# A list scheduler given other instruction costs, router constants moved to an earlier due time, and the state rows of heads 3 to 5 exchanged

## The chip, the core and the metric

The kernel runs on one core of a Trainium2 chip. The metric is the device time of one execution in microseconds. Five engines work side by side, each on its own queue in program order: PE (matrix multiplications; PEld is its weight load), DVE (vector), ACT (scalar, with function tables), POOL (which here issues the indirect transfers) and SP (which issues almost all other transfers). Engines wait for one another by semaphores.

## The reference

The reference is one linear recurrence with a complex decay per head, followed by two mixtures of experts. Cut to what matters:

```
# 4 x 8 heads, 768 steps, 48 channels; a is complex, its size clipped at 0.999
for t in range(768):
    S_re, S_im = a_re*S_re - a_im*S_im + outer(k[t], v[t]),  a_re*S_im + a_im*S_re
    y[t] = q[t] @ S_re
x = y, heads side by side                                  # 3072 tokens x 384
# MoE 1: a token with x @ w_skip > 0 goes to the best of 8 experts
x += gate * (relu(x @ w1[e]) @ w2[e]),  e = argmax(x @ w_gate)
# MoE 2: every token goes to the best of 8 experts
logits = normalise(x) @ normalise(expert_emb).T / tau
out = gate * (relu(x @ w1[e]) @ w2[e]),  e = argmax(logits) # w1 384 x 1024, w2 1024 x 384
```

## The kernel before

**How it is recorded.** No instruction is issued where it is written. Each is recorded in a `Plan` (L72 to 240) with its engine, a modelled cost, what it reads and writes, and a due time; a transfer also has a modelled time in flight. Dues are carried backwards through the dependences. Then forward and backward list-scheduling passes run over the modelled times, and the order with the shortest modelled end is issued. So a modelled cost is not a time on the chip, but it decides the order in every engine's queue. Modelled idle time of PE is filled with dummy matrix multiplications (`keep_warm`, L431).

**The recurrence (about 0 to 250 us).** The work is cut into eight groups `g` (a batch and half of its sequence) and 24 chunks of 128 tokens. `feat(g)` (L440 to 552) loads the decay (tile RI) and q with k (tile QK, L463). On ACT and DVE it turns the decay into running sums (scans, L471) and into sine and cosine. Two multiplications (L529) give tile PR (the cosine part of q and k) and, in place, tile QK (the sine part). Both are then moved on chip (L540) into tile ST, where a head's cosine part and sine part stand under one another in 96 partitions. PIECES lists the five moves for each part: heads 0 to 2, heads 3 to 5, and three for heads 6 and 7. `chunk(k)` (L575 to 690) multiplies on PE from ST (W, L593), masks on DVE (WM, L596), turns k round (KT, L604), makes the output (L620) and the state (L629), and then x with the first router's scores (L640 to 646).

**Between.** Router constants (`consts`, L771 to 812): five small loads, the expert embeddings' norms on DVE, two tiny matrix multiplications (L805, L806) and three small DVE operations (L809 to 811), which the first chunk's scores need. `route` ranks tokens and scatters them by POOL into a table `tab` in device memory (L733); `slots` (L758) reads back two lanes of it (ts1f and LANE for MoE 1; ts2f and LANE for MoE 2).

**The experts.** `gather` (L995) has POOL gather up to 128 rows of x into one of twelve buffers xg. PE turns them round (L919), DVE or ACT copy them (L925, L926), h = relu(x w1) is L950 with L954 and L958, o = h w2 is L982. Weights are loaded by SP (w1 at L884, w2 at L887) into a few buffers r and split into high and low parts (ACT L893, DVE L894). MoE 1 scatters its result into xd (L1036), MoE 2 into out (L1231). In MoE 2, `select` (DVE, L1150 to 1153) computes each expert's slot indices, and the expert number goes to SP by a cast on POOL (WE, L873).

```
PIECES = [((0, 3), 0, 0, 0, 48), ((3, 6), 0, 48, 0, 48), ((6, 8), 0, 96, 0, 32), ((6, 7), 2, 96, 32, 16), ((7, 8), 2, 112, 32, 16)]
# (heads, block, source partition, row within the part, rows)
for x, ks, a0 in ((vp, kp, 0), (vc, kqk, 1)):      # PR is part 0, QK part 1
    ...  d[a0 * D + o : a0 * D + o + m, ...] <- x[p0 : p0 + m, ...]     # D = 48
```

Of the kernel before, what the change touches and what calls it, by code (L numbers as in the profile page):

```python
# [15 lines left out]
ALU = mybir.AluOpType  # L16
AX = mybir.AxisListType
# [4 lines left out]
P = 128  # L22
# [47 lines left out]


def cells(g):  # L72

    return PARTS.get(g, ((0, NC),))


class Plan:
# [9 lines left out]

    def add(self, eng, cost, fn, r=(), w=(), due=1e9, lat=0.0, tab=None, phase=None, dram=None, after=()):
# [20 lines left out]
        self.ops.append([eng, cost, fn, deps, due, lat, tab, self.bias, dram, self.hold])  # L109

    def lag(self, i, j):
        a, b = self.ops[i], self.ops[j]
        if b[3][i] is None:
            return 0.0
        if a[5]:
            return self.START + a[5] + self.END
        if a[0] != b[0]:
            return self.CROSS
        return self.SAME if b[3][i] and a[0] != "pe" else 0.0
# [16 lines left out]
    def forward(self, due, succ):  # L136
# [11 lines left out]
        while len(out) < n:  # L148
# [29 lines left out]
            if o[5]:  # L178
                dma = max(dma, end + self.START) + o[5]
                done = dma + self.END  # L180
                late = done - end - (self.START + o[5] + self.END)
# [11 lines left out]
    def backward(self, ends, succ):  # L193
# [10 lines left out]
        while count < n:  # L204
# [15 lines left out]
            if o[5]:  # L220
                flight = self.START + o[5]
                late = max(lanes[eng][0] + flight + self.END, dma + flight)
                if o[8]:
                    a, b = o[8]
                    late = max([late] + [touched.get((a, c), -9.0) + flight + self.END for c in self.CLASH[b]])
# [48 lines left out]
def kernel(  # L274
# [112 lines left out]
    def dve(n, fn, r, w, due=1e9):  # L387
        plan.add("dve", 0.06 + 1.05e-3 * n, fn, r, w, due)

    def pe(us, fn, r, w, due=1e9):  # L390
        plan.add("pe", us, fn, r, w, due)

    def dma(us, fn, r, w, due=1e9, dram=None, cost=0.47):
        plan.add("sp", cost, fn, r, w, due, us, dram=dram)

    def pool(us, fn, r, w, due=1e9, dram=None):
        plan.add("pool", 1.05, fn, r, w, due, us, dram=dram)

# [34 lines left out]
    def feat(g):  # L433
# [72 lines left out]
        def back(i, j):  # L506
# [30 lines left out]
            for x, ks, a0 in ((vp, kp, 0), (vc, kqk, 1)):  # L537
                for y, (h, bk, p0, o, m) in enumerate(PIECES):
                    nh = h[1] - h[0]
                    dma(MOVE * wide(j) / P * nh * m / D, lambda x=x, a0=a0, h=h, nh=nh, bk=bk, p0=p0, o=o, m=m: nc.sync.dma_start(  # L540
                        d[a0 * D + o : a0 * D + o + m, 2 * h[0] * w : 2 * h[1] * w],
                        x[p0 : p0 + m, 2 * bk * w : 2 * (bk + nh) * w]),
                        ks(j), [("st", g % 2, y, a0, i) for i in range(j.start, j.stop)], cost=0.64)
# [134 lines left out]
    def route(nm, n, nr, lg, klg, sel, ksel, c0, pay, kpay, inval, pcol, due, late=(), pt0=0):  # L678
# [52 lines left out]
        for i in range(n):  # L731
# [3 lines left out]
                in_=pay[:, i, 0:W], in_offset=None, bounds_check=2 * E * N - 1, oob_is_err=False),  # L735
                [("ix", nm)] + klg + kpay + span(["ti"], range(2), (0, E // 2), [lane]), [("tab", nm, i)] + ([("tabB", lane)] if late else []), due, (f"t{lane}", "all"))
        tabs.append([("tab", nm, i) for i in range(n)])
# [20 lines left out]
    def slots(t, view, src, ks, key, due, kf=()):  # L758
        parts = [view(x) for x in t["l"]]
        for lane in range(2):  # L760
            dma(0.2, lambda lane=lane: nc.sync.dma_start(parts[lane], src(lane)), ks, [(key, lane), *kf], due, (f"t{lane}", "read"))
        dve(math.prod(parts[0].shape[1:]), lambda: nc.vector.tensor_tensor(view(t["f"]), parts[0], parts[1], op=ALU.add), [(key, 0), (key, 1)], [(key, 2), *kf], due)
# [64 lines left out]
    feat(0)()  # L827
    pe(0.5, lambda: nc.tensor.matmul(PS[7][:, 384:512], lhsT=PR[:, 0:P], rhs=maskT, start=True, stop=True), [("pr", 0, 0)], [], -100.0)
    consts()
    feat(1)()  # L830
    backs = {}
# [98 lines left out]
    def h_part(m, e, cap, c0, c1, due, raw=False):  # L930
# [4 lines left out]
        cut = [(c0, cap - rem), (cap - rem, c1)] if c1 == cap and rem else [(c0, c1)]  # L935
        us = 0.66 * w / P if raw else 9 * max(w, 250) / 2370
        for f in range(NF):
# [25 lines left out]
    def o_part(m, e, cap, c0, c1, due, finish, raw=False):  # L963
# [3 lines left out]
        for t in range(c0 // P, -(-c1 // P)):  # L967
# [3 lines left out]
            for f0, f1 in ((0, 6), (6, 8)):  # L971

                def mm(f0=f0, f1=f1, t=t, n=n, po=po):
# [11 lines left out]

                pe(0.488 * (f1 - f0) * (1 if n == P else 0.667), mm,
                   span([name], range(f0, f1), [min(t, 2)], range(2) if n == P else (0, 2)) + span(["w2"], range(f0 // 2, f1 // 2), range(2)),
# [3 lines left out]
    def gather(m, e, t, n, idx, kidx, kx, due, rows=N + 1):  # L991
        s = slot(m, e, t)
        if rows <= N:
# [3 lines left out]
            in_offset=IO(ap=idx.bitcast(U32), axis=0), bounds_check=rows - 1, oob_is_err=False),  # L997
            kidx + kx + ["w"], [("xg", s), ("xgd", m, e, t)], due, ("x", "read") if rows > N else None)

# [3 lines left out]
    def moe1():  # L1003
# [20 lines left out]
        def finish(e, t, n, po, kpo, due):  # L1024
# [13 lines left out]
                in_=T["o"][ox], in_offset=None, bounds_check=N - 1, oob_is_err=False),  # L1038
                [("o", ox)] + kx, [("xs", e, t)], due + 4, ("x", "all"))
            bank = 3 if t % 2 else 6  # L1040
# [104 lines left out]
    def select(p, h, kin, due):  # L1145
# [6 lines left out]
        dve(144, lambda: V.tensor_reduce(f, tmp, axis=AX.X, op=ALU.add), kin + [("tmp", h)], [("f2", p % 3, h)], due)  # L1152
        dve(2, lambda: V.tensor_scalar(
# [53 lines left out]
    def moe2():  # L1207
# [12 lines left out]
        def finish(p, t, n, po, kpo, due):  # L1220
# [5 lines left out]
            else:  # L1226
# [6 lines left out]
                in_=T["o"][ox][0:n], in_offset=None, bounds_check=N - 1, oob_is_err=False),  # L1233
                [("o", ox)], [("out", p, t)], due + 4)

# [7 lines left out]
        def gates2(p, t0, t1, k, due):  # L1243
# [6 lines left out]
            for t, r in tiles(p)[t0:t1]:  # L1250
                x = slot(1, p, t)
                act(508, lambda t=t, r=r, x=x: nc.scalar.activation(  # L1252
                    T["xg"][x][0:r], T["xg"][x][0:r], AF.Square, accum_out=SQ2[0:r, i0 + t : i0 + t + 1]),
# [316 lines left out]
```

## Time and profile before

| what | value |
|---|---|
| runs | 709.4, 713.12, 712.95 us; median 712.95 |
| profiled execution, its own time | 710.47 us |
| its span, first to last instruction | 708.7 us |
| mean granted clock of PE | 0.945 |
| PE busy | 631.4 us (89%) |
| DVE, ACT, POOL busy | 459.9 (65%), 401.5 (57%), 163.9 (23%) us |
| moved by DMA | 115.91 MB, mean 164 GB/s |

The profiled execution lasted 1.8 us more than its span. A high share of PE over the whole says little about a single stretch: the recurrence, the two passages into the mixtures and the mixtures themselves have different limits, so the rows below go by stretches. [...]

### The profile page before, as it was taken

Reading aid. Unit: us, or ns where it says so; the run is one execution under the profiler, and the core shown is the slowest. Engines: PE = TensorE matmul, PEld = TensorE weight load, DVE = VectorE, ACT = ScalarE, POOL = GpSimd, SP = SyncE. Lnnn points to the kernel's source line nnn. Section 1 sums busy time; section 2 is a strip of 40 time slices with the busy share of each in tenths; the row PEclk is TensorE's granted clock in tenths of the full one; section 3 lists DMA queues with packets and bytes.
Section 4 is the critical chain, followed back from the end, with each engine's and each line's share of the span. In section 5 each row is a group of like instructions: output and inputs, shape, how many; then the busy total and the mean of one; then the engine's idle time right before and its main releaser. Section 6 shows DMA issues by size and latency. Waiting matters only on the chain.

```text
span 708.7 us, 12836 instructions
## 1 busy us (share of the span) xinstructions
PE 631.4 (89%) x4734; PEld 606.7 (86%) x4734; DVE 459.9 (65%) x1058; ACT 401.5 (57%) x695; POOL 163.9 (23%) x171
## 2 busy tenths in 40 slices
PE   0478999799989987799999999859999999999995
PEld 0478988788979877799999999859999999999995
DVE  4997899699986463667676747726836536374350
ACT  6986979587976532555555544215654535555340
POOL 5000000000344225212332134544141413102101
PEclk9996999699999998799999999857999999999998
DMA  9866997599566777756455331494554433023001
GB/s 296 307 172 158 297 247 183 151 220 232 129 155 156 264 193 258 242 195 215 138 143 152 103 107 20 82 347 143 179 198 143 156 112 134 33 89 115 30 10 36
DMA packets 52103, 115.91 MB, mean 164 GB/s; under 512 B 22909, under 2 KB 27139, under 8 KB 49346
## 3 DMA queue, kind: packets, MB, share of 16 engines
q1 hardware_dynamic: 43682, 93.94, 46.2%
q0 software_dynamic: 8352, 21.09, 9.4%
q8 instruction: 39, 0.64, 0.4%
q14 instruction: 30, 0.25, 0.1%
HBM read 83.30 MB, written 14.09 MB: 137 GB/s over the span
## 4 chain that ended last, share of the span: by engine, by line
PE 58%; DMA 13%; DVE 11%; issue 10%; SPq 3%; POOL 2%; ACT 2%; POOLq 0%; DVEq 0%; ACTq 0%
PE PS L982 23%; PE PS L950 23%; DMA ST<-QK 4%; DMA tab<-LG,ixa 3%; PE PS L919 2%; PE PS L593 2%; DMA ST<-PR 2%; DMA QK<-in_qk 2%; POOL tab L733 2%; DMA LANE<-tab 1%; SPq L540 1%; PE PS L431 1%; DVE WM L596 1%; PE PS L620 1%; DVE RI L471 1%
## 5 line engine op out<-in xcount | busy, mean ns | idle before, releaser
L950 PE MATMUL PS<-x,w 128*128 128x256 f32 (+4 forms) x1152 | 188.5, 323 | 7.8 <-DVE zn L748 7.8
L982 PE MATMUL PS<-w,h 128*128 128x384 f32 (+1 forms) x1032 | 190.9, 340 | 0.0
L950 PEld LDWEIGHTS PS<-x,w 128*128 128x128 f32 x1152 | 179.4, 200 | 9.6 <-issue 7.9
L982 PEld LDWEIGHTS PS<-w,h 128*128 128x128 f32 (+1 forms) x1032 | 177.5, 185 | 2.7
L954 ACT ACTIVATE h<-PS 128x256 fp32r<-128x256 f32 (+5 forms) x136 | 58.0, 428 | 119.5 <-PE PS L950 97.6
L958 DVE SCALAR_TENSOR_TENSOR h<-PS,h 128x256 fp32r<-128x256 f32 (+4 forms) x184 | 67.7, 391 | 76.1 <-ACT h L954 57.4
L593 PE MATMUL PS<-ST 96*128 96x128 f32 x384 | 60.5, 303 | 14.2 <-DMA ST<-QK 9.7
L593 PEld LDWEIGHTS PS<-ST 96*128 96x128 f32 x384 | 52.6, 210 | 17.9 <-DMA ST<-QK 10.2
L1231 POOL DMA_INDIRECT out<-o,ts2i x30 | 29.7, 991 | 165.0 <-ACT o L1225 118.7
L900 DVE TENSOR_TENSOR w<-r,w 128x768 fp32r<-128x768 f32 x64 | 58.4, 951 | 13.3 <-ACT w L899 10.1
L926 DVE TENSOR_TENSOR x<-PS,x 128x256 fp32r<-128x256 f32 (+4 forms) x48 | 23.1, 485 | 56.7 <-ACT x L925 52.0
L899 ACT CAST w<-r 128x768 fp32r<-128x768 f32 x64 | 50.5, 832 | 15.5 <-PE PS L982 8.3
L894 DVE TENSOR_TENSOR w<-r,w 128x1024 fp32r<-128x1024 f32 x45 | 53.5, 1219 | 5.0 <-ACT w L893 5.0
L925 ACT CAST x<-PS 128x256 fp32r<-128x256 f32 (+4 forms) x48 | 20.3, 426 | 54.1 <-PE PS L919 47.9
L431 PE MATMUL PS<-cst 128*128 128x128 f32 x302 | 45.4, 300 | 3.0 <-DVE cs L810 1.8
L893 ACT CAST w<-r 128x1024 fp32r<-128x1024 f32 x45 | 45.0, 1050 | 0.3 <-issue 0.2
L431 PEld LDWEIGHTS PS<-cst 128*128 128x128 f32 x302 | 41.5, 213 | 4.2 <-DVE cs L810 1.9
L995 POOL DMA_INDIRECT xg<-xd,ts2i x30 | 34.7, 1157 | 35.3 <-ACT xg L1252 17.6
L558 POOL DMA_DIRECT2D VT<-in_v x8 | 4.6, 572 | 162.2 <-PE PS L620 112.9
L596 DVE TENSOR_TENSOR WM<-PS,cst 128x512 f32<-128x512 f32 x48 | 32.2, 679 | 12.3 <-PE PS L593 12.1
L620 PE MATMUL PS<-WM,VT 128*48 128x128 f32 x384 | 37.9, 288 | 1.1 <-DVE WM L596 0.8
L733 POOL DMA_INDIRECT tab<-LG,ixa x24 | 27.8, 1158 | 47.6 <-DMA tab<-LG,ixa 23.3
(209 smaller groups left out, 960.7 us busy)
## 6 DMA issues: line engine op xcount, KB each, us to landing
r<-in_w1a SPq DMA_DIRECT2D x24, 512.0 KB
r<-in_w2a SPq DMA_DIRECT2D x32, 384.0 KB
r<-in_w1b SPq DMA_DIRECT2D x24, 512.0 KB
r<-in_w2b SPq DMA_DIRECT2D x32, 384.0 KB
RI<-in_ri SPq DMA_DIRECT2D x6, 1152.0 KB
QK<-in_qk SPq DMA_DIRECT2D x6, 1152.0 KB
ST<-PR SPq DMA_DIRECT2D x12, 432.0 KB
ST<-QK SPq DMA_DIRECT2D x12, 432.0 KB
```

The costliest lines, as they stand in the source:

```text
L431: nc.tensor.matmul(PS[7][:, 384:512], lhsT=ident, rhs=maskT, start=True, stop=True)
L593: nc.tensor.matmul(wt[:, h % 4, :], lhsT=st(1, h), rhs=st(0, h), start=True, stop=True)
L620: nc.tensor.matmul(py[64 * j : 64 * j + D, p, :], lhsT=w, rhs=r, start=(x == 0), stop=(x == 1 or i == 0))
L733: pool(0.2, lambda i=i, lane=lane: nc.gpsimd.indirect_dma_start(out=tab[lane][:, :], out_offset=IO(ap=ix[:, i : i + 1].bitcast(U32), axis= ...
L893: act(F, lambda s=s: nc.scalar.copy(T["w1"][q % 2][0][s], T["r1"][q % 2][s]), [("r1", q % 2, j), "L"], [k + (0,)])
L894: dve(F, lambda s=s: nc.vector.tensor_tensor(T["w1"][q % 2][1][s], T["r1"][q % 2][s], T["w1"][q % 2][0][s].bitcast(F32), op=ALU.subtract), ...
L899: act(2 * DM, lambda s=s: nc.scalar.copy(T["w2"][0][s], T["r2"][s]), [("r2", j)], [k + (0,)])
L900: dve(2 * DM, lambda s=s: nc.vector.tensor_tensor(T["w2"][1][s], T["r2"][s], T["w2"][0][s].bitcast(F32), op=ALU.subtract), [("r2", j), k + ...
L950: nc.tensor.matmul(ph, lhsT=l, rhs=r, start=(i == 0), stop=(i == len(seq) - 1))
L954: act(w, lambda f=f, ph=ph: nc.scalar.activation(T[name][:, f, o0 : o0 + w], ph, AF.Relu), [("ps", f % 3), "w" if name == "hA" else "L"], ...
L958: dve(b - a, lambda f=f, ph=ph, a=a, b=b, o=o: nc.vector.scalar_tensor_tensor(T[name][:, f, o : o + b - a], ph[:, a - c0 : b - c0], 0.0, T ...
L982: nc.tensor.matmul(po if n == P else po[0 : 2 * stride], lhsT=x, rhs=w[:, f, :], start=(f == 0 and i == 0), stop=(f == NF - 1 and i == len ...
```

## The change

Five things change, most of them numbers of the scheduler's model.

1. `row(h, k)`: for heads 3 to 5 the cosine part goes to rows 48 to 95 of ST and the sine part to rows 0 to 47. The other heads stay: cosine in rows 0 to 47, sine in rows 48 to 95. Both factors of each product are moved alike, so the products are the same.
2. `consts()` is recorded with a bias of -60 on its due times.
3. The modelled costs: a POOL issue 0.6 instead of 1.05 and an indirect one 1.3; a DVE operation 0.07 + 1.045e-3 n instead of 0.06 + 1.05e-3 n; the selections 250 and 240 elements instead of 144; h_part 9 * (w / 2400 + 0.0135) instead of 9 * w / 2370; o_part 0.52 for each step instead of 0.488; a square of ACT 430 instead of 508.
4. A new term `more` in the modelled time in flight: 1.2 for a table scatter and a slot load, 2.0 for a gather.
5. What follows from these numbers: another order in all five queues, with the same real work. Dummy multiplications also fall in other places.

```diff
+def row(h, k):
+    return (1 - k if h[0] == 3 else k) * D
...
         if a[5]:
-            return self.START + a[5] + self.END
+            return self.START + a[5] + self.END + a[10]
...
-        plan.add("dve", 0.06 + 1.05e-3 * n, fn, r, w, due)
+        plan.add("dve", 0.07 + 1.045e-3 * n, fn, r, w, due)
...
-    def pool(us, fn, r, w, due=1e9, dram=None):
-        plan.add("pool", 1.05, fn, r, w, due, us, dram=dram)
+    def pool(us, fn, r, w, due=1e9, dram=None, cost=0.6, more=0.0):
+        plan.add("pool", cost, fn, r, w, due, us, dram=dram, more=more)
...
-                        d[a0 * D + o : a0 * D + o + m, 2 * h[0] * w : 2 * h[1] * w],
+                        d[row(h, a0) + o : row(h, a0) + o + m, 2 * h[0] * w : 2 * h[1] * w],
...
+    plan.bias = -60.0
     consts()
+    plan.bias = 0.0
...
-        us = 0.66 * w / P if raw else 9 * max(w, 250) / 2370
+        us = 0.66 * w / P if raw else 9 * (max(w, 250) / 2400 + 0.0135)
...
-            kidx + kx + ["w"], [("xg", s), ("xgd", m, e, t)], due, ("x", "read") if rows > N else None)
+            kidx + kx + ["w"], [("xg", s), ("xgd", m, e, t)], due, ("x", "read") if rows > N else None, 1.3, 2.0)
...
-        dve(144, lambda: V.tensor_tensor(
+        dve(250, lambda: V.tensor_tensor(
```

Three places in the queues. The first is the beginning of PE's queue (dg and tt are the router constants, cst a constant, the rows of L431 dummies). Before, the rows that led up to the constants, in the middle of the first chunks' work:

```order
L593 MATMUL PS_101<-ST_108 128x128 x4
L604 MATMUL PS_103<-cst,ST_108 128x96 x4
L431 MATMUL PS_107<-cst 128x128 x3
L593 MATMUL PS_100<-ST_108 128x128 x4
L620 MATMUL PS_104<-WM_112,VT_120 48x128 x4
L620 MATMUL PS_104<-WM_113,VT_120 48x128 x4
L604 MATMUL PS_102<-cst,ST_108 128x96 x4
L593 MATMUL PS_100<-ST_108 128x128 x4
L805 MATMUL PS_107<-dg,cst 128x8
L806 MATMUL PS_107<-tt,cst 128x1
```

and now, from the head of the queue (line numbers are 5 higher here):

```order
L810 MATMUL PS_107<-dg,cst 128x8
L811 MATMUL PS_107<-tt,cst 128x1
L436 MATMUL PS_107<-cst 128x128 x9
L833 MATMUL PS_107<-cst,PR 128x128
L436 MATMUL PS_107<-cst 128x128 x41
L609 MATMUL PS_102<-cst,ST_108 128x96 x4
L598 MATMUL PS_100<-ST_108 128x128 x4
```

The two matrix multiplications of the constants moved from behind the first chunk's work to the head of the queue.

The second is SP's queue at the entry of MoE 1, where the weights of the next expert (w1a into r) meet the slot loads from the table. Before:

```order
L645 DMA xd<-XT_123 128x384
L884 DMA r_2255<-in_w1a 128x1024 x3
L761 DMA ts1f<-tab_64 128x7x9
L761 DMA LANE<-tab_65 128x7x9
L761 DMA ts1f<-tab_64 128x7x9
L761 DMA LANE<-tab_65 128x7x9
L884 DMA r_2255<-in_w1a 128x1024 x3
```

and now:

```order
L650 DMA xd<-XT_123 128x384
L891 DMA r_2241<-in_w1a 128x1024 x5
L766 DMA ts1f<-tab_64 128x7x9
L766 DMA LANE<-tab_65 128x7x9
L766 DMA ts1f<-tab_64 128x7x9
L766 DMA LANE<-tab_65 128x7x9
L891 DMA r_2241<-in_w1a 128x1024
```

Two of the later weight loads, which need a buffer that a split (L894) sets free, now stand ahead of the slot loads.

The third is POOL's queue at the entry of MoE 2 (the last table scatters, the scatter of finished rows to out, the gathers). Before:

```order
L733 DMA tab_64<-LG,ixb_203 49152x17
L733 DMA tab_65<-LG,ixb_204 49152x17
L1231 DMA out<-o_2036,ts2i 3072x384
L995 DMA xg_2030<-xd,ts2i 128x384
L995 DMA xg_2031<-xd,ts2i 64x384
L995 DMA xg_2034<-xd,ts2i 128x384
L995 DMA xg_2035<-xd,ts2i 64x384
L995 DMA xg_2032<-xd,ts2i 128x384
```

and now:

```order
L738 DMA tab_64<-LG,ixb_203 49152x17
L738 DMA tab_65<-LG,ixb_204 49152x17
L1238 DMA out<-o_1986,ts2i 3072x384
L1238 DMA out<-o_1987,ts2i 3072x384
L1002 DMA xg_1980<-xd,ts2i 128x384
L1002 DMA xg_1981<-xd,ts2i 64x384
L1002 DMA xg_1982<-xd,ts2i 128x384
L1002 DMA xg_1983<-xd,ts2i 128x384
```

A second scatter to out came ahead of the first gather; the weights' cast WE still follows the sixth gather.

## Rows read from the trace of the kernel before

**Rows 1.** Windows: busy us (count) of PE, PEld, DVE, ACT, POOL; clock, DMA share, GB/s.

```profile
20.00:40.00 20.00, 12.01 (x82) 12.01 (x83) 19.96 (x25) 19.03 (x22) 0.00 (x0) 1.00 0.76 273
...
120.00:140.00 20.00, 15.13 (x103) 14.15 (x102) 13.55 (x18) 12.48 (x14) 0.53 (x1) 0.66 0.71 176
...
250.00:300.00 50.00, 40.08 (x277) 38.39 (x277) 26.10 (x92) 19.83 (x47) 18.68 (x18) 0.86 0.74 233
300.00:340.00 40.00, 40.00 (x299) 39.85 (x299) 26.18 (x53) 20.77 (x38) 9.65 (x10) 1.00 0.58 186
...
440.00:498.00 58.00, 47.99 (x255) 44.68 (x254) 33.25 (x131) 19.77 (x50) 26.41 (x26) 0.76 0.64 188
498.00:700.00 202.00, 202.00 (x1136) 195.79 (x1134) 101.32 (x249) 97.61 (x202) 40.70 (x39) 1.00 0.31 104
```

**Rows 2.** Waits of DVE from 20 to 200 us: total, times, longest.

```profile
DVE WM L596 <- PE PS L593: 8.5, 5, 2.8
DVE QK L515 <- ACT T L501: 3.4, 2, 1.7
DVE rt L809 <- PE PS L806: 2.1, 1, 2.1
```

**Rows 3.** Chain that ended last, 0 to 300 us: start, microseconds, what.

```profile
46.11 6.01 DMA ST<-PR
...
142.40 8.75 DMA ST<-PR
...
153.51 8.74 DMA ST<-QK
...
280.70 5.06 issue
```

**Rows 4.** PE at the entry of MoE 2, idle time before in brackets.

```profile
459.29 5.43 PE L950 MATMUL PS<-x,w 128*128 128x192 f32 x27
472.49 3.91 PE L950 MATMUL PS<-x,w 128*128 128x192 f32 x17 [7.77 <-DVE zn L748]
```

**Rows 5.** Window of the long idle time there.

```profile
461.00:472.00 11.00, 3.72 (x21) 3.55 (x20) 0.08 (x1) 0.33 (x1) 7.50 (x10) 0.66 0.99 371
```

**Rows 6.** SP's moves into ST in two groups: start, microseconds, what.

```profile
112.96 4.83 SPq L540 DMA_DIRECT2D ST<-PR  x4
117.89 3.63 SPq L540 DMA_DIRECT2D ST<-QK  x3
...
141.15 5.57 SPq L540 DMA_DIRECT2D ST<-PR  x5
```

**Rows 7.** Windows of 4 us around those moves, and one with loads.

```profile
116.00:120.00 4.00, 4.00 (x55) 3.71 (x54) 4.00 (x6) 2.44 (x7) 0.00 (x0) 1.00 1.00 171
120.00:124.00 4.00, 2.84 (x27) 2.65 (x26) 4.00 (x8) 4.00 (x4) 0.53 (x1) 1.00 0.99 209
144.00:148.00 4.00, 4.00 (x56) 3.69 (x54) 2.31 (x3) 3.97 (x5) 0.00 (x0) 1.00 0.96 171
148.00:152.00 4.00, 3.57 (x34) 3.30 (x34) 4.00 (x8) 3.49 (x5) 0.00 (x0) 1.00 0.95 230
...
80.00:84.00 4.00, 3.88 (x41) 3.69 (x40) 3.90 (x2) 4.00 (x8) 0.00 (x0) 1.00 1.01 397
```

**Rows 8.** SP at the entry of MoE 1: slot loads, then weights.

```profile
260.56 0.38 SPq L761 DMA_DIRECT2D ts1f<-tab  x1
...
263.75 13.02 SPq L884 DMA_DIRECT2D r<-in_w1a  x6
```

**Rows 9.** POOL at the entry of MoE 1, idle time before in brackets.

```profile
271.89 1.03 POOL L995 DMA_INDIRECT xg<-xd,ts1i  x1 [6.40 <-DMA xd<-o,ts1i]
```

**Rows 10.** POOL's first two gathers of MoE 2.

```profile
450.50 1.26 POOL L995 DMA_INDIRECT xg<-xd,ts2i  x1 [0.44 <-issue]
452.07 0.98 POOL L995 DMA_INDIRECT xg<-xd,ts2i  x1 [0.31 <-DVE ts2i L1153]
```

**Rows 11.** ACT's second output of MoE 2.

```profile
452.47 0.58 ACT L1225 ACTIVATE o<-PS,ts2g 128x384 f32<-128x384 f32 x1 [3.65 <-issue]
```

More of the change, by code (lines that the diff above doesn't have):

```diff
@@ L86, in __init__, with add @@
         self.bias, self.hold, self.phases = 0.0, 0.0, {}
-    def add(self, eng, cost, fn, r=(), w=(), due=1e9, lat=0.0, tab=None, phase=None, dram=None, after=()):
+    def add(self, eng, cost, fn, r=(), w=(), due=1e9, lat=0.0, tab=None, phase=None, dram=None, after=(), more=0.0):
         i = len(self.ops)
@@ L108, in add @@
             self.phases.setdefault(phase, []).append(i)
-        self.ops.append([eng, cost, fn, deps, due, lat, tab, self.bias, dram, self.hold])
+        self.ops.append([eng, cost, fn, deps, due, lat, tab, self.bias, dram, self.hold, more])
     def lag(self, i, j):
@@ L179, in forward @@
                 dma = max(dma, end + self.START) + o[5]
-                done = dma + self.END
-                late = done - end - (self.START + o[5] + self.END)
+                done = dma + self.END + o[10]
+                late = done - end - (self.START + o[5] + self.END + o[10])
                 lanes[eng] = lanes[eng][1:] + [done]
@@ L221, in backward @@
                 flight = self.START + o[5]
-                late = max(lanes[eng][0] + flight + self.END, dma + flight)
+                late = max(lanes[eng][0] + flight + self.END + o[10], dma + flight)
                 if o[8]:
                     a, b = o[8]
-                    late = max([late] + [touched.get((a, c), -9.0) + flight + self.END for c in self.CLASH[b]])
+                    late = max([late] + [touched.get((a, c), -9.0) + flight + self.END + o[10] for c in self.CLASH[b]])
                 if late > t:
@@ L387, in dve, with dma @@
     def dve(n, fn, r, w, due=1e9):
-        plan.add("dve", 0.06 + 1.05e-3 * n, fn, r, w, due)
+        plan.add("dve", 0.07 + 1.045e-3 * n, fn, r, w, due)
     def pe(us, fn, r, w, due=1e9):
         plan.add("pe", us, fn, r, w, due)
-    def dma(us, fn, r, w, due=1e9, dram=None, cost=0.47):
-        plan.add("sp", cost, fn, r, w, due, us, dram=dram)
-    def pool(us, fn, r, w, due=1e9, dram=None):
-        plan.add("pool", 1.05, fn, r, w, due, us, dram=dram)
+    def dma(us, fn, r, w, due=1e9, dram=None, cost=0.47, more=0.0):
+        plan.add("sp", cost, fn, r, w, due, us, dram=dram, more=more)
+    def pool(us, fn, r, w, due=1e9, dram=None, cost=0.6, more=0.0):
+        plan.add("pool", cost, fn, r, w, due, us, dram=dram, more=more)
     st_s, el_s, st_w, st_l = (ExitStack() for _ in range(4))
@@ L735, in route @@
                 in_=pay[:, i, 0:W], in_offset=None, bounds_check=2 * E * N - 1, oob_is_err=False),
-                [("ix", nm)] + klg + kpay + span(["ti"], range(2), (0, E // 2), [lane]), [("tab", nm, i)] + ([("tabB", lane)] if late else []), due, (f"t{lane}", "all"))
+                [("ix", nm)] + klg + kpay + span(["ti"], range(2), (0, E // 2), [lane]), [("tab", nm, i)] + ([("tabB", lane)] if late else []), due, (f"t{lane}", "all"), 1.3, 1.2)
         tabs.append([("tab", nm, i) for i in range(n)])
@@ L760, in slots @@
         for lane in range(2):
-            dma(0.2, lambda lane=lane: nc.sync.dma_start(parts[lane], src(lane)), ks, [(key, lane), *kf], due, (f"t{lane}", "read"))
+            dma(0.2, lambda lane=lane: nc.sync.dma_start(parts[lane], src(lane)), ks, [(key, lane), *kf], due, (f"t{lane}", "read"), more=1.2)
         dve(math.prod(parts[0].shape[1:]), lambda: nc.vector.tensor_tensor(view(t["f"]), parts[0], parts[1], op=ALU.add), [(key, 0), (key, 1)], [(key, 2), *kf], due)
@@ L984, in mm @@
                                 stop=(f == NF - 1 and i == len(seq) - 1))
-                pe(0.488 * (f1 - f0) * (1 if n == P else 0.667), mm,
+                pe(0.52 * (f1 - f0) * (1 if n == P else 0.667), mm,
                    span([name], range(f0, f1), [min(t, 2)], range(2) if n == P else (0, 2)) + span(["w2"], range(f0 // 2, f1 // 2), range(2)),
@@ L1038, in finish @@
                 in_=T["o"][ox], in_offset=None, bounds_check=N - 1, oob_is_err=False),
-                [("o", ox)] + kx, [("xs", e, t)], due + 4, ("x", "all"))
+                [("o", ox)] + kx, [("xs", e, t)], due + 4, ("x", "all"), 1.3)
             bank = 3 if t % 2 else 6
@@ L1149, in select @@
         oh = OH[:, p, :].rearrange("p (a b e) -> p a b e", a=1, b=1).to_broadcast([P, 2, E + 1, E])
[L1150 removed]
+        dve(250, lambda: V.tensor_tensor(
             tmp, src, oh, op=ALU.mult), kin + [("oh2", min(p, 1))], [("tmp", h)], due)
[L1152 removed]
+        dve(240, lambda: V.tensor_reduce(f, tmp, axis=AX.X, op=ALU.add), kin + [("tmp", h)], [("f2", p % 3, h)], due)
         dve(2, lambda: V.tensor_scalar(
@@ L1233, in finish @@
                 in_=T["o"][ox][0:n], in_offset=None, bounds_check=N - 1, oob_is_err=False),
-                [("o", ox)], [("out", p, t)], due + 4)
+                [("o", ox)], [("out", p, t)], due + 4, None, 1.3)
         def gathers(p, due, t0=0):
@@ L1251, in gates2 @@
                 x = slot(1, p, t)
-                act(508, lambda t=t, r=r, x=x: nc.scalar.activation(
+                act(430, lambda t=t, r=r, x=x: nc.scalar.activation(
                     T["xg"][x][0:r], T["xg"][x][0:r], AF.Square, accum_out=SQ2[0:r, i0 + t : i0 + t + 1]),
```

## Prediction

> **What bounds the kernel now.** I read the windows by stage first, because the whole hides the stages [rows 1]. In the mixtures PE is the bound: 40.00 of 40 us from 300 to 340 and 202.00 of 202 from 498 to 700, at full clock. The change takes no real work out of them, so nothing can be won there but dummies. From 20 to 40 us DVE is the bound (19.96 of 20). From 120 to 140 nothing is: PE 15.13, DVE 13.55, at a mean clock of 0.66. The two passages, 250 to 300 and 440 to 498, keep PE busy 40.08 of 50 and 47.99 of 58 us, at clocks of 0.86 and 0.76.
>
> The waits of DVE from 20 to 200 us come next [rows 2]: 8.5 us in five waits for the first product of a chunk (WM behind L593), 3.4 us for ACT, and 2.1 us for the router's tiny products (rt behind L806). The first product needs tile ST, and the chain of waits says the same: moves into ST lie in it from 46.11 us on, with 6.01, 8.75 and 8.74 us in the rows shown [rows 3].
>
> In the passages the chain ends in PE standing for something that no instruction explains: 5.06 us at 280.70 [rows 3], 7.77 us before 472.49 [rows 4]. In the second, the eleven microseconds from 461 have DVE busy 0.08 and ACT 0.33 us, while the DMA engines are busy 0.99 at 371 GB/s [rows 5]: gathers and weight loads together.
>
> **The change part by part.** The profiled execution took 710.47 us, its span 708.7 us. The sum is made against 710.47; the median of the runs is 2.5 us higher and their lowest 1.1 us lower, so one profile does not fix the level better than that.
>
> *Rows of heads 3 to 5.* Before, SP issued the cosine moves (PR, all into rows 0 to 47) as one batch and the sine moves (QK, all into rows 48 to 95) as another [rows 6]. The windows of 4 us over them show DMA engines equally busy, 0.95 to 1.00, but with different yields [rows 7]: 171 GB/s in both windows that hold PR moves, 209 and 230 GB/s in the two after them, when QK moves follow; 397 GB/s with loads alone. So a busy engine does not mean a given rate, and the target rows seem to decide it. A group's PR batch is two pieces of 48 x 2304, one of 32 x 1536 and two of 16 x 768 numbers of 4 bytes, 1.18 MB: 6.9 us at 171 GB/s, 5.4 us at the mean of 220, a gain of 1.5 us. Other transfers share the windows and blur the difference, so I take 2 us a group.
> [...]
> A landing that is earlier by 2 us helps only where someone waits. The stretch from 120 to 140 alone has 6.45 us of idle DVE [rows 1], so that most of the five waits of 8.5 us [rows 2] hang on one landing; I estimate that they shrink by its 2 us, what lies elsewhere by 2 us too, and by 0.5 us more as PE's half clock in that stretch ends sooner. That makes -4.5 us, with bounds of 0 (DVE is the bound and fills the time anyway) and -8.5 (all five waits). QK moves lose nothing by it: their batch now has the same mix of rows.
>
> *Router constants.* Their products moved to the head of PE's queue. The wait of 2.1 us [rows 2] goes, and DVE's small operations for them move ahead of the first multiplications (L529). There DVE is the bound [rows 1], and they push these back by as much; but it is the same work, only earlier. I take -1.5 us; bounds -2.1 and +1 (the first landing of 46.11 to 52.12 us later [rows 3]).
>
> *Entry of MoE 1.* SP now issues two more loads of 512 KB ahead of the slot loads. At 397 GB/s [rows 7] that is 1.3 us each, 2.6 us on slots that were issued from 260.56 [rows 8]. But the gathers did not wait for slots: the first was issued at 271.89 after 6.40 us of waiting for a scatter to xd [rows 9], which lay beside six weight loads that held SP 13.02 us [rows 8]. Of these loads, two now come earlier. I take 0, bounds +2.6 (the slots' delay in full) and -2.6 (the scatter lands earlier by as much).
>
> *Entry of MoE 2.* POOL's first gather was issued at 450.50 [rows 10]. It now stands behind the second scatter to out, whose rows ACT ends at 452.47 + 0.58 = 453.05 [rows 11]. With 1.0 us for the scatter, as for a gather, and the gap of 0.3 us [rows 10] the gather comes at 454.4, 3.9 us later. PE's first expert product, 459.29 [rows 4], came 7.2 us after the second gather at 452.07; part of that was DVE, busy with selections that will by then be done, so I count +2 us of the 3.9. Behind the gather wait all later gathers and the cast that gives SP the expert number, so the burst of loads moves back about 4 us as well, and the long idle time with it. Bounds: -7.8 (the idle time of 7.77 us goes) and +9.3 (third rival).
>
> *Modelled costs.* They cost nothing on the chip. The rest of the order in the mixtures changes little, and PE covers it [rows 1]: 0, give or take 1 us.
>
> Sum: -4.5 - 1.5 + 0 + 2 + 0 = -4.0 on 710.47. **Forecast 706.5 us.** About 0.5%, 3.6 us, is what a measurement of this kernel can tell from no change: below 709.4 counts as faster than the median of 712.95, above 716.5 as slower.
>
> **Rivals.**
> *Phase one gains nothing.* The moves' yield hangs on the transfers that share the windows rather than on rows, or DVE fills the time. For it: DVE is busy 19.96 of 20 us [rows 1]; the 171 and 209 GB/s lie only a fifth apart [rows 7]. Against it: the chain holds ST moves of over 8 us [rows 3], and DVE does wait for them. Then -1.5 + 2, 711 us.
> [...]
> *The idle time at 461 us goes or shrinks.* Gathers, moved later by 4 us, and weight loads no longer fill the engines together. For it: the order around is another. Against it: POOL issues the same six gathers before the cast, and the weights follow the cast as before. Then -4.5 - 1.5 - 7.8, and about 1.7 us less at half clock afterwards (an estimate): 695 us.
> *Slower: PE meets the idle time with nothing done.* The first gather comes at 454.4. If the engines then fill up before its rows are turned, the 27 products of 5.43 us that ran from 459.29 [rows 4] run after the idle time, at half clock: 3.9 + 5.4 = +9.3 us. This decides if the first expert product starts after the stall does. With a gain of 2 to 3 us in the first phase it gives 710.5 + 9.3 - 2.5 = 717 us. For it: eleven idle microseconds are already there [rows 5], and the change takes nothing away from the burst. Against it: the burst hangs on the same queue and moves back as well.
>
> **How the numbers follow.** Forecast 0.45, no gain in phase one 0.22, idle time gone 0.13, slower 0.20. Within the forecast the bounds above give 701 to 711. Faster is most of the forecast (0.36), all of the idle time's case (0.13) and a little of the second (0.04): 0.53. Slower is most of the last rival (0.16) and 0.06 from the upper bounds of both entries coming together in the other cases: 0.22. Within 0.5% is what is left: 0.25. The range reaches from the 695 of the second rival to the 717 of the third, 695 to 717, with about 2 in 10 outside.
>
> **What would show it.** PR moves: windows over them above 200 GB/s, and landings in the chain under 7 us. Constants: no wait of rt behind L811. WM's waits for L598 under 5.5 us in all from 20 to 200. Entry of MoE 1: the first gathers of the burst not later, against the end of the recurrence, than 271.89. Entry of MoE 2: first gather 4 us behind its place, relative to the last products of MoE 1, and the idle time still about 8 us. The prediction is wrong if the landings are as long as before, or if the idle time before MoE 2 changes by more than 3 us in either direction.

## The result, and the profile after

The change made the kernel slower: 718.77 us (median of 20 runs) against 710.6 us for before in the same comparison, ratio 1.0108 [1.0079, 1.0137]. The forecast was 706.5 us, in a range of 695 to 717. The profiled execution spans 717.8 us instead of 708.7.

The ratios leave out runs that lie more than 1.5% above a kernel's fastest, and as runs of this kernel scatter by 2 to 3%, that drops many of before's in one comparison and few in the next; so the difference of the medians of all runs stands beside each ratio. By it the changed kernel is 8.2 us slower here, and 8.4 us in a second comparison.

The windows by stage of the changed kernel, columns as in [rows 1]:

```profile
20.00:40.00 20.00, 4.91 (x26) 4.83 (x27) 19.92 (x39) 17.36 (x22) 0.00 (x0) 1.00 0.52 204
120.00:140.00 20.00, 19.39 (x217) 18.18 (x217) 18.26 (x26) 17.06 (x25) 0.54 (x1) 1.00 0.88 260
160.00:180.00 20.00, 17.18 (x131) 16.32 (x131) 11.48 (x19) 10.90 (x17) 2.12 (x2) 0.66 0.88 222
250.00:300.00 50.00, 39.69 (x317) 36.77 (x314) 27.57 (x105) 21.11 (x49) 19.31 (x18) 0.92 0.77 237
300.00:340.00 40.00, 40.00 (x274) 39.92 (x275) 25.77 (x47) 20.95 (x39) 5.66 (x5) 0.93 0.62 199
440.00:498.00 58.00, 47.73 (x318) 44.88 (x318) 34.38 (x153) 19.72 (x56) 24.70 (x27) 0.85 0.48 140
498.00:700.00 202.00, 202.00 (x1132) 194.87 (x1132) 108.63 (x270) 102.75 (x208) 42.72 (x42) 1.00 0.34 117
```

The mixtures are as full as before. The recurrence is not: the stretch with idle DVE, 120 to 140 us before, now lies at 160 to 180 us and is deeper (11.48 busy). Two windows over the same 180 us of the recurrence, first of before, then of the changed kernel, sum it up:

```profile
20.00:200.00 180.00, 156.71 (x1556) 147.25 (x1556) 163.98 (x237) 148.49 (x191) 10.89 (x10) 0.92 0.80 209
```

```profile
20.00:200.00 180.00, 146.69 (x1446) 138.61 (x1448) 154.92 (x222) 141.33 (x179) 15.13 (x15) 0.91 0.72 200
```

DVE did 9.1 us less work in the same time. Its waits there, as in [rows 2]:

```profile
DVE WM L601 <- PE PS L598: 15.8, 7, 6.3
DVE T L501 <- ACT T L500: 4.7, 1, 4.7
DVE T L504 <- ACT T L502: 1.7, 1, 1.7
DVE RI L497 <- ACT RI L489: 1.4, 2, 0.7
```

The wait for the router's products is gone, as foreseen; the waits of WM grew from 8.5 to 15.8 us, and a wait of 4.7 us for ACT is new. That one comes from SP's queue, where a load of RI stands behind moves into ST (start, us, what):

```profile
37.95 3.18 SPq L545 DMA_DIRECT2D ST<-PR  x5
41.17 0.58 SPq L468 DMA_DIRECT2D RI<-in_ri  x1
```

Before had such a load behind moves as well, at 32.45 us. But the moves wait for the first multiplications, and these came 10.0 us later than before (first row before, second row the changed kernel):

```profile
26.98 0.95 DVE L529 TENSOR_TENSOR PR<-QK,RI 128x768 f32<-128x768 f32 x1
```

```profile
36.98 0.95 DVE L534 TENSOR_TENSOR PR<-QK,RI 128x768 f32<-128x768 f32 x1
```

ACT then waits for the load, and DVE for ACT:

```profile
52.44 1.16 ACT L488 ACTIVATE T<-RI 128x1152 f32<-128x1152 f32 x1 [3.16 <-DMA RI<-in_ri]
```

```profile
54.78 1.36 DVE L501 SCALAR_TENSOR_TENSOR T<-T,T 128x1152 f32<-128x1152 f32 x1 [4.70 <-ACT T L500]
```

The end of the recurrence shows in the last table scatter that MoE 1's slots need, on POOL: first before, then the changed kernel, with the changed kernel's first gather of the burst.

```profile
258.94 0.97 POOL L733 DMA_INDIRECT tab<-LG,ixa  x1 [3.17 <-DVE hA L958]
```

```profile
270.15 1.00 POOL L738 DMA_INDIRECT tab<-LG,ixa  x1 [2.20 <-DMA xg<-xd,ts1i]
...
279.02 1.05 POOL L1002 DMA_INDIRECT xg<-xd,ts1i  x1 [3.67 <-DVE gm L1182]
```

The scatter is 11.2 us late, the gather 7.1 us later than [rows 9]. At the entry of MoE 2 POOL shows, first the last table scatter of before, then the changed kernel, with its PE below:

```profile
440.00 0.97 POOL L733 DMA_INDIRECT tab<-LG,ixb  x1 [0.32 <-issue]
```

```profile
450.07 0.97 POOL L738 DMA_INDIRECT tab<-LG,ixb  x1 [0.30 <-DVE h L965]
458.64 0.97 POOL L1238 DMA_INDIRECT out<-o,ts2i  x1 [7.59 <-ACT o L1232]
462.87 0.97 POOL L1238 DMA_INDIRECT out<-o,ts2i  x1 [3.26 <-ACT o L1232]
464.15 1.05 POOL L1002 DMA_INDIRECT xg<-xd,ts2i  x1 [0.30 <-DVE ts2i L1160]
```

```profile
478.06 0.77 PE L926 MATMUL PS<-cst,xg 128*128 128x128 f32 x2 [7.97 <-issue]
478.76 1.22 PE L436 MATMUL PS<-cst 128*128 128x128 f32 x4
479.63 0.72 PE L957 MATMUL PS<-x,w 128*128 128x192 f32 x2
481.20 8.18 PE L957 MATMUL PS<-x,w 128*128 128x192 f32 x34 [0.85 <-issue]
```

The second scatter, issued 4.2 us after the first, now stands ahead of the first gather and holds it until 464.15 us, as the third place of the order said, and PE now meets its idle time (7.97 us) before its first expert product, where [rows 4] had 27 products ahead of it. Even so, nearly the whole loss is there before the mixtures begin: the changed kernel is 11.2 us behind at the last table scatter for MoE 1, 10.1 us at that for MoE 2 (450.07 against 440.00) and 9.1 us at the end of the span.

### The profile page after: what moved, and what is told of

Read it like the earlier page. It is cut to its first block, busy times and chain, and to the rows that moved or that the text cites. A ratio compares the mean times of both kernels' runs of the same rounds, so it can differ in the third digit from the quotient of the medians.

```text
span 717.8 us, 12862 instructions
## 1 busy us (share of the span) xinstructions
PE 629.0 (88%) x4748; PEld 605.1 (84%) x4748; DVE 460.8 (64%) x1058; ACT 400.9 (56%) x693; POOL 165.8 (23%) x171
## 4 chain that ended last, share of the span: by engine, by line
PE 67%; DMA 10%; DVE 9%; issue 4%; ACT 4%; SPq 3%; another core or an unknown queue 1%; POOL 1%; DVEq 0%; POOLq 0%; ACTq 0%
PE PS L957 25%; PE PS L989 25%; DMA ST<-QK 6%; PE PS L598 4%; PE PS L926 3%; PE PS L625 2%; SPq L545 2%; PE PS L634 2%; DVE T L476 1%; PE PS L609 1%; DVE PR L534 1%; PE PS L1060 1%; PE PS L436 1%; DMA RI<-in_ri 1%; DVE RI L476 1%
## 5 line engine op out<-in xcount | busy, mean ns | idle before, releaser
L957 PE MATMUL PS<-x,w 128*128 128x256 f32 (+4 forms) x1152 | 186.2, 320 | 0.9 <-issue 0.9
L957 PEld LDWEIGHTS PS<-x,w 128*128 128x128 f32 x1152 | 177.2, 196 | 3.4 <-issue 1.1
L598 PE MATMUL PS<-ST 96*128 96x128 f32 x384 | 58.2, 304 | 5.7 <-DMA ST<-QK 3.3
L436 PE MATMUL PS<-cst 128*128 128x128 f32 x316 | 47.5, 295 | 2.1 <-issue 1.4
L436 PEld LDWEIGHTS PS<-cst 128*128 128x128 f32 x316 | 43.1, 208 | 3.6 <-issue 2.4
L738 POOL DMA_INDIRECT tab<-LG,ixa x24 | 30.4, 1266 | 67.7 <-DVE sel L661 21.8
L1002 POOL DMA_INDIRECT xg<-xd,ts2i x30 | 33.9, 1131 | 34.8 <-PE PS L957 10.8
L1043 POOL DMA_INDIRECT xd<-o,ts1i x16 | 19.3, 1207 | 87.4 <-DVE o L1040 58.7
```

The lines of the kernel that those rows point to most:

```text
L436: nc.tensor.matmul(PS[7][:, 384:512], lhsT=ident, rhs=maskT, start=True, stop=True)
L598: nc.tensor.matmul(wt[:, h % 4, :], lhsT=st(1, h), rhs=st(0, h), start=True, stop=True)
L957: nc.tensor.matmul(ph, lhsT=l, rhs=r, start=(i == 0), stop=(i == len(seq) - 1))
L1002: pool(0.6, lambda: nc.gpsimd.indirect_dma_start(out=T["xg"][s][0:n, :], out_offset=None, in_=xd[0:rows, :], in_offset=IO(ap=idx.bitcast(U ...
```

## The experiments

All kernels of one group ran on one chip beside before. Theory A at the start was: rows do little, the loss is the new order of the recurrence. Theory B: the rows. Theory C: the entries of the mixtures. Theory K came later: PE's lower clock.

Most kernels take their order from a written list, so that only chosen parts move. The list gives, for each recorded step, its index and the idle time to be filled with dummies, so the dummies go along with the order:

```diff
-        for i, new, t, end in self.order():
+        for i, gap in struct.iter_unpack("<Hh", zlib.decompress(base64.b85decode(LIST))):
```

In `after_out_moved` below, whose list differs from the changed kernel's order in one place of POOL's queue, PE and SP run the changed kernel's instructions one for one. "Cut at the recurrence" means: the steps that one planner places up to the last chunk's store to xd, in its order, then all others in the order of the other.

**First group** (before 688.7 us). `rows_only` is before with the rows, `after_rows_back` the changed kernel with the old rows; neither changes the order.

```diff
-                        d[a0 * D + o : a0 * D + o + m, 2 * h[0] * w : 2 * h[1] * w],
+                        d[row(h, a0) + o : row(h, a0) + o + m, 2 * h[0] * w : 2 * h[1] * w],
```

> The order of before, instruction by instruction, with row() alone: the state rows of heads 3 to 5 exchanged. Theory A (the loss of 8 us is the new order of the recurrence's first 50 us, and rows do little): within 3 us of before, in either direction. Theory B (the loss comes from the rows, two batches that now load both halves at once): slower by 6 to 9 us. My prediction's own term: faster by 4.5 us, PR windows above 200 GB/s and landings in the chain under 7 us.

> The changed kernel with the old rows, its order unchanged. Theory A: as slow as the changed kernel, 7 to 9 us over before, or more if the rows help. Theory B: back at before, within 3 us.

Measured: `rows_only` 686.68 us, 2.0 us under before, ratio 0.9945 [0.9907, 0.9984]; `after_rows_back` 706.41 us, 17.7 us over, 1.0258 [1.0209, 1.0307]. The rows help in both orders, and theory B falls. Two windows of `rows_only` over the same PR moves as in [rows 7]:

```profile
115.00:119.00 4.00, 4.00 (x55) 3.71 (x54) 4.00 (x6) 2.44 (x7) 0.00 (x0) 1.00 0.91 220
...
143.00:147.00 4.00, 4.00 (x55) 3.69 (x55) 2.01 (x3) 3.97 (x5) 0.00 (x0) 1.00 0.71 190
```

Against 171 GB/s at 1.00 and 0.96 busy, they yield 220 and 190 GB/s at less busy engines. Such a window also hangs on what else it holds: those over the changed kernel's PR moves, from 95, 146, 166 and 200 us, yield 190, 145, 269 and 151 GB/s. The time from issue to landing tells more. With the same order in the recurrence, the median of the 432 KB pieces is 8.3 us for PR and 9.1 for QK with the old rows (`after_rows_back`), and 6.5 and 7.1 with the new ones in `changed_again` below (6.7 and 7.3 in `after_out_moved`, 8.2 and 7.2 in `h_rec_after`).

The two other kernels of the group start with the order of before and go on with that of the changed kernel: `h_phase1_before` is cut at the recurrence, `h_early_before` at 55 modelled us.

> Rows exchanged; the whole recurrence, up to the last chunk's scores, in the order of before, and the rest in the order of the changed kernel. Theory A: the loss of the recurrence is gone, 0 to +3 us against before, from the later first gather of MoE 2. Theory C (the loss is made at the two entries): still 6 us or more over before.

> Rows exchanged; only the first 55 modelled us in the order of before (to the first chunk's first products), and everything after it in the order of the changed kernel. Theory A: first chunk's scores near 69 us instead of 83, and most of the loss gone: within 4 us of before. If the order of the later recurrence is at fault: the first chunk early, yet the last table scatter of MoE 1's slots still near 270 us and the time 6 us or more over before.

Measured: 692.73 us, 4.0 over, 1.0039 [1.0001, 1.0077]; and 696.08 us, 7.4 over, 1.0117 [1.0069, 1.0166]. So by the medians about half of the loss goes with the order of the recurrence. `h_early_before` multiplies as early as before (26.84 us), but its first chunk's scores come only at 82.08 us (before 69.17): the order behind the cut gives the lead away, so this kernel does not tell what an early first chunk is worth.

**Second group** (before 690.95 us). The changed kernel again; its recurrence with the rest of before; before up to the last table scatter for MoE 2; and one instruction moved in POOL's queue, so that its order there is:

```diff
 L1238 DMA out<-o_1986,ts2i 3072x384
-L1238 DMA out<-o_1987,ts2i 3072x384
 L1002 DMA xg_1980<-xd,ts2i 128x384
 ...
 L1002 DMA xg_1977<-xd,ts2i 32x384
+L1238 DMA out<-o_1987,ts2i 3072x384
```

> The changed kernel as it is, beside the three below on one chip. Expected 1.1% over before, some 7.5 us, by the first measurement.

> Rows exchanged; the recurrence in the order of the changed kernel, everything after it in the order of before. If the loss is made in the recurrence (theory A): 4 to 8 us over before. If it is made in the passages and the mixtures (theory C): at most 1 us over before, or under it by the gain of the rows.

> Rows exchanged; the order of before up to the last table scatter for MoE 2, then the order of the changed kernel. The same kernel with the cut behind the recurrence was 0.4% over before, with the order of before throughout 0.55% under it. If the entry of MoE 2 and what follows makes that percent: again 0 to 0.5% over. If the entry of MoE 1 makes it (weights ahead of slot loads): 0.5% under.

> The changed kernel with one instruction moved: the second scatter to out stands behind the tenth gather of MoE 2, as it did before. By my term for this entry: first gather 3 to 4 us earlier, PE's first expert product 2 us earlier, time 2 us under the changed kernel. If the first gather is not what the passage waits for: within 1 us of it.

Measured: `changed_again` 699.35 us, 8.4 over, 1.0209 [1.0136, 1.0282]. `h_rec_after` 699.3 us, 8.4 over, 1.0204 [1.0119, 1.0288]: the recurrence of the changed kernel alone brings the whole loss. `h_moe1_before` 692.53 us, 1.6 over, 1.0106 [1.0027, 1.0185]; against its own before that is 3.6 us more than `rows_only`, from which it differs behind the last table scatter for MoE 2 alone. `after_out_moved` 695.07 us, 4.1 over, 1.0064 [1.0007, 1.0121]: 4.3 us less than `changed_again`, where I had counted 2. POOL in `changed_again`, then in `after_out_moved`:

```profile
444.83 0.97 POOL L738 DMA_INDIRECT tab<-LG,ixb  x1 [0.34 <-DVE ixb L730]
...
459.43 1.05 POOL L1002 DMA_INDIRECT xg<-xd,ts2i  x1 [0.30 <-DVE ts2i L1160]
```

```profile
440.34 0.97 POOL L802 DMA_INDIRECT tab<-LG,ixb  x1 [0.34 <-DVE ixb L794]
...
451.18 1.05 POOL L1066 DMA_INDIRECT xg<-xd,ts2i  x1 [0.78 <-issue]
```

The first gather moved from 14.6 to 10.8 us behind the last table scatter. From that scatter to the end of the span, the six traces of groups one, two and four that have the changed order there take 256.3 to 258.3 us, the three with that of before 253.7 to 254.3, and `after_out_moved` 253.2. The parts don't add up: with either half of before (`h_phase1_before`, `h_rec_after`) the loss is 4 and 8 us, with both 2 us of gain.

**Third group** (before 710.15 us). One line of the change undone; dummies in front of products that wait for ST; two weight loads moved back behind the slot loads; and the last two together.

```diff
-    plan.bias = -60.0
     consts()
-    plan.bias = 0.0
```

```diff
-L891 DMA r_2241<-in_w1a 128x1024 x5
+L891 DMA r_2241<-in_w1a 128x1024 x3
 L766 DMA ts1f<-tab_64 128x7x9
 ...
-L891 DMA r_2241<-in_w1a 128x1024
+L891 DMA r_2241<-in_w1a 128x1024 x3
```

> The changed kernel without the bias of -60 on the router constants; the planner lays out everything anew. If the bias is what makes the recurrence slow (first multiplication at 37 us instead of 27): first chunk's scores before 75 us and 4 us or more under the changed kernel, which stood 8.4 us over before by the medians. If another of the numbers does it as well: still 5 us or more over before.

> The changed kernel with eleven dummy products in front of each of seven first products of the groups 3, 4 and 6, where PE waits for ST. Theory K (PE's granted clock falls in these waits and the recurrence runs on at half clock, 0.50 over 160 to 180 us): clock above 0.8 in that stretch, last chunk's scores 4 us or more earlier, time 4 us or more under the changed kernel (8.4 us over before). If the lost time is the late rows of ST themselves: no gain, or 1 to 3 us slower by the dummies.

> The changed kernel with the second scatter to out behind the tenth gather of MoE 2, and the two early weight loads behind the slot loads of MoE 1, as before. The first edit alone took 4.3 us off the changed kernel by the medians. If the weight loads cost the 2.4 us that the two cuts leave for MoE 1: 1 to 2 us over before. If they cost nothing: 4 us over before.

> The two moves of the kernel above and the dummies of warm_wait. By theory K and both moves together: 0 to 4 us under before. If dummies do nothing: as the kernel with both moves.

Measured: `after_no_bias` 700.43 us, 9.7 us **under** before, 0.9868 [0.9811, 0.9925]. `warm_wait` 723.21 us, 13.1 over, 1.0195 [1.0145, 1.0245]. `after_both_moved` 714.01 us, 3.9 over, 0.9977 [0.9931, 1.0022]: by the median no better than the one move, by the ratio better (1.0064 there). `both_warm` 715.81 us, 5.7 over, 1.0075 [1.0035, 1.0115]. What the early weight loads cost stays open: from the last table scatter for MoE 1 to that for MoE 2 `warm_wait` takes 179.5 us, and `both_warm`, with the loads moved back, 174.8; but `changed_again` and `after_out_moved`, which do not differ there, are 3.9 us apart as well.

The first is the turn of the study. Its first chunk's scores come later than in any kernel so far, at 99.48 us (first row; 83.39 in the changed kernel, second row; 69.17 in before, third):

```profile
99.48 1.07 PE L645 MATMUL PS<-wrs,XTT 128*128 128x113 f32 x8
```

```profile
83.39 1.07 PE L645 MATMUL PS<-wrs,XTT 128*128 128x113 f32 x8
```

```profile
69.17 1.07 PE L640 MATMUL PS<-wrs,XTT 128*128 128x113 f32 x8
```

and yet its recurrence ends before those of the other two, the last table scatter being at 252.93 us. Its DVE is as busy as that of before (window, then waits):

```profile
20.00:200.00 180.00, 154.19 (x1552) 144.75 (x1552) 164.70 (x238) 153.93 (x196) 23.81 (x17) 0.94 0.79 213
```

```profile
DVE LG L651 <- PE PS L645: 4.0, 2, 2.7
DVE PR L534 <- ACT RI L529: 3.1, 1, 3.1
...
DVE WM L601 <- PE PS L598: 1.0, 1, 1.0
```

```profile
252.93 0.99 POOL L738 DMA_INDIRECT tab<-LG,ixa  x1 [0.31 <-issue]
```

Behind WM it waits 1.0 us, where before waits 8.5 and the changed kernel 15.8.

**Fourth group** (before 690.81 us). The order of before with only the constants moved to the places that the changed kernel gives them, rows exchanged (`consts_early`); before with the bias alone; fewer dummies; and `after_no_bias` with the scatter to out moved.

```diff
+    plan.bias = -60.0
     consts()
+    plan.bias = 0.0
```

> Rows exchanged, the order of before, with the router constants alone moved to the places that the changed kernel gives them (their products at the head of PE's queue, their small operations among the first 36 us of DVE); nothing else changes place. If constants that come early cost nothing (my term was -1.5 us): 0 to 4 us under before, like the rows alone (2 us under). If they themselves push the recurrence back: 4 us or more over before.

> Before with the bias of -60 on the constants and nothing else: old rows, old costs, another order drawn by the planner. If the bias leads the planner astray whatever the costs: 5 us or more over before. If the loss was one draw among many: anywhere from 5 under to 5 over; DVE's waits behind WM from 20 to 215 us then tell it, 11 us before, 16 to 18 in the changed kernel, 1 without the bias.

> The changed kernel with dummies only in front of four products of the groups 3 and 4. With three more in front of group 6 the clock stayed at 1.00 from 100 to 180 us and group 6 was multiplied at 193.4 instead of 197 us, but DVE then waited 4.6 us for a ranking product behind the dummies. By theory K: 3 to 4 us under the changed kernel (4 to 5 over before). If half clock is only a sign of the wait: no better than the changed kernel (8 over before).

> The changed kernel without the bias and with the second scatter to out behind the tenth gather of MoE 2. The first alone stood 9.7 us under before; the second took 4.3 us off the changed kernel. If the two are independent: 12 to 14 us under before.

Measured: `consts_early` 688.48 us, 2.3 under, 0.998 [0.9942, 1.0017], like the rows alone: early constants cost nothing that shows in the time. In its trace, though, DVE waits 15.9 us behind WM from 20 to 215 us, and the last table scatter for MoE 1 stands at 262.36 us. `bias_only` 692.14 us, 1.3 over, 1.0012 [0.9967, 1.0057]: with the old costs the bias does no harm that shows, though DVE's waits behind WM are long there. `nobias_out_moved` 679.39 us, 11.4 under, 0.9877 [0.9816, 0.9938]. `warm_g34` 698.73 us, 7.9 over, 1.0127 [1.009, 1.0164]: no better than the changed kernel, so theory K gets no support. The stretch from 160 to 180 us in `changed_again`, then in `warm_g34`, and the longest waits of DVE in the latter:

```profile
160.00:180.00 20.00, 19.53 (x112) 18.57 (x114) 9.47 (x18) 10.52 (x16) 3.09 (x3) 0.50 0.79 195
```

```profile
160.00:180.00 20.00, 20.00 (x215) 19.59 (x214) 13.24 (x23) 12.85 (x19) 2.12 (x2) 1.00 0.75 197
```

```profile
DVE WM L665 <- PE PS L662: 9.9, 8, 2.6
DVE T L565 <- ACT T L564: 4.9, 1, 4.9
DVE w8s L793 <- PE PS L500: 4.6, 1, 4.6
```

The clock went from 0.50 to 1.00 and the waits behind WM from 17.6 us (20 to 215 us of `changed_again`) to 9.9, but DVE then waited 4.6 us for a ranking product that had come to stand behind the dummies. The test does not refute theory K either. In that stretch of `changed_again` PE was busy 19.53 of 20 us, and DVE's longest wait behind WM passed while PE worked without a gap at 0.50, through products that stood ahead in its queue:

```profile
173.04 0.69 DVE L601 TENSOR_TENSOR WM<-PS,cst 128x512 f32<-128x512 f32 x1 [6.26 <-PE PS L598]
```

```profile
165.12 2.69 PE L634 MATMUL PS<-VT,KT 128*96 128x48 f32 x16
...
170.93 2.08 PE L598 MATMUL PS<-ST 96*128 96x128 f32 x8
```

In `warm_g34` three blocks of dummies took 2.70, 2.62 and 2.65 us of PE there, and the scores product behind them started at 177.65 us instead of 177.12: the dummies used up what the full clock gave back.

**Fifth group** (before 710.33 us). The recurrence in the order drawn without the bias, then the order of the changed kernel, or of before.

> Rows exchanged; the recurrence in the order that the planner draws without the bias, everything after it in the order of the changed kernel. If the order of the recurrence is the whole loss: 8 to 12 us under before, as the kernel without the bias (9.7 us under), where the changed kernel stands 8.4 us over. If part of it lies behind the recurrence: between the two.

> The same recurrence, everything after it in the order of before. The cuts so far put the rest of the changed order at 4 to 6 us of loss (second scatter to out ahead of the first gather): 11 to 15 us under before. If that loss hangs on the late recurrence: as the kernel above.

Measured: `rec_nobias_rest_changed` 704.69 us, 5.6 under by the medians; its ratio, 1.0003 [0.9946, 1.006], does not show it. `rec_nobias_rest_before` 698.09 us, 12.2 under, 0.987 [0.9819, 0.9921]. So by the medians another order of the recurrence, with the same rows and the rest kept, takes the changed kernel from 8 us over to 6 us under: 14 of the 18 us between it and `after_no_bias`. By the ratios (1.0108 and 1.0209 for the changed kernel, 0.9868 for `after_no_bias`) it is about half. The rest of the changed order costs 6.6 us against that of before, in line with the 6.0 us between `h_phase1_before` and `rows_only`.

The change without the bias is the simplest version that beats both kernels; the three best (0.9868, 0.9877, 0.987) can't be told apart.

The traces bear the swaps out. With the new rows, the last table scatter for MoE 1 stands at 250.5, 258.2 and 259.2 us where the recurrence has the order of before (`rows_only`, `h_moe1_before`, `h_phase1_before`), at 266.1 to 270.2 in five traces with the changed one, and at 246.7 to 256.9 in four with the order drawn without the bias. One order alone varies by 4 to 10 us between traces, so a single pair of them would not have settled it.

## Why the prediction was wrong

The forecast was -4.0 us, the result +8.2. Term by term:

- **Rows of heads 3 to 5**, forecast -4.5: right in sign and mechanism. By themselves -2.0 us in the order of before (0.55% by the ratio), some -9 us in that of the changed kernel (17.7 against 8.4 over before, on two chips). The pieces land about 2 us sooner, as counted (medians with the same order in the recurrence: PR 6.5 us instead of 8.3, `changed_again` against `after_rows_back`), but those of QK do so too (7.1 instead of 9.1), for which I had counted no gain. That landings in the chain would fall under 7 us was wrong: the chain of the changed kernel still holds five pieces of ST<-QK of 8.3 to 9.5 us, and its PR windows lie at 145 to 269 GB/s, not all above 200. What it is in the target rows that brings the landings forward no run shows.
- **Router constants**, forecast -1.5: the failed step. I priced the instructions that the bias names, and moved alone they cost nothing that shows: `consts_early` is 2.3 us under before, `rows_only` 2.0, while the wait of rt, 2.1 us in before, is 0.2 us in `bias_only`. What I put at nothing, for the recurrence without a reason, is the order that the bias sets off: a due time in a list scheduler moves everything that is placed after it. I compared the queues at three places and walked neither DVE's nor SP's through the 24 chunks. The runs show 8.4 us of loss from the recurrence of the changed kernel alone (`h_rec_after`), and 12.2 us of gain from the one that the planner draws without the bias (`rec_nobias_rest_before`), with the same rest. The upper bound of +1 us on the first landing was wrong too, as the first multiplication came 10.0 us later. But a late start is not the loss: `after_no_bias` has its first chunk's scores 16 us later still and wins.
- **Modelled costs**, forecast 0: also part of that step. With the new costs, the new rows and no bias the planner draws an order 9.7 us faster than before; with bias, old costs and old rows, one that is level. Neither number is good or bad by itself.
- **Entry of MoE 1**, forecast 0: not contradicted. From its last table scatter to that for MoE 2 the changed kernel takes 179.9 us, before 181.1; what the early weight loads cost within that stays open.
- **Entry of MoE 2**, forecast +2: right mechanism, too small. The first gather came 3.6 us later relative to the last table scatter (14.1 against 10.5 us). Moving one scatter back took 4.3 us off by the medians, and the traces of groups one, two and four put the place at about 3 us. In the first comparison, where before has a long idle time of its own here, the two traces do not show it: 267.7 us from that scatter to the end, 268.7 before.
- **The rivals**: the slower one, with 0.20, named 717 us and this place; its point was reached in the changed kernel's trace (the idle time lay ahead of the first expert product). That its number lies so near the result is luck: in the second group the changed kernel loses as much (8.4 us) without that idle time, and with the scatter moved 4.1 us remain. Its eleven idle microseconds [rows 5] were those of DVE and ACT; PE was idle for 7.3 of them.

That the order of the recurrence makes the loss is shown by the swaps. How it does so is argued from the traces. A WM that stood in DVE's queue before its product was there held what stood behind it: in the changed kernel DVE waited 6.25 us for the WM of 175.76 us, and the scans behind it ran from 178.96 us on. In the changed kernel's traces products were late for two reasons: moves into ST that landed late (PE waited 2.33 us for one before 107.55 us and 2.82 before 163.38), and PE's own queue at half clock (the 6.26 us above). The order that wins queues chunk work late and waits 1.0 us behind WM; the order that loses waits 15.8 us, and its DVE did 9.1 us less by 200 us, against 11.2 us lost by the end. But `bias_only` and `consts_early` have 19.4 and 15.9 us behind WM and are level with before, which this reading does not explain, and the one attempt to take such a wait away by itself (`warm_g34`) put dummies in PE's way.

## What to carry to other kernels

When a change feeds a list scheduler, the instructions it names are the smallest part of it: walk the in-order queue of the bound engine through the whole stage, and look for operations that wait, for a transfer or for another engine's queue, with independent work behind them. An earlier first result is no gain by itself; the fastest kernels here were those with the latest first chunk (scores at 99.48 us in `after_no_bias`). Dummies that kept the clock at 1.00 took time in the queue themselves (8.0 us of PE in `warm_g34`). Test each number of such a change by undoing it alone, and fix the order in a list to separate an edit from the order that it sets off.

## What the runs showed of the hardware

The same kernel took 689 to 691 us on the chips of three groups and 710 us on those of the other comparisons. The long idle time of PE at the entry of MoE 2 goes with the chip: on the faster ones, the waits of PE in 425 to 500 us are at most 3.9 us in all in each of the twelve kernels traced, against 7.4 to 10.8 us in the eight on the others. The changed kernel is among the twelve, and its first expert products run there as

```profile
465.75 0.71 PE L436 MATMUL PS<-cst 128*128 128x128 f32 x4
466.21 4.25 PE L957 MATMUL PS<-x,w 128*128 128x192 f32 x36
```

without the 7.97 us of standing that the same program had on the other chip. What differs between the chips stays open, but it lies behind the recurrence: the changed kernel's last table scatter for MoE 1 came at 270.15 us on the one and at 270.19 on the other, and the rest took 447.7 and 431.7 us. From 160 to 180 us PE's granted clock was 1.00 with the dummies of `warm_g34`, instead of 0.50 in `changed_again`, and the time did not follow (7.9 and 8.4 us over before); they took 8.0 us of PE there themselves. What the half clock itself costs in that stretch is not shown.
